# One list that orders the start of an attention and mixture-of-experts kernel, written anew, with freer table changes and later scatters

## The chip, the cores and the metric

The kernel runs on one core of a Trainium2 chip. The metric is device time in microseconds (us) of one execution. Before the change the median of three runs is 699.96 us (699.73 to 700.44). Engine names are those of the profile: PE is TensorE with its matmuls (PEld its weight loads), DVE is VectorE, ACT is ScalarE, POOL is GpSimd, SP is SyncE, which here only issues transfers.

## The reference

Two layers follow each other: a gated linear attention with a complex decay per step, and on its output a mixture of eight experts of which each token takes two.

```python
def _attn_ref(q, k, v, a_re, a_im):            # batch 4, heads 8, steps 768, width 48
    mag = np.sqrt(a_re * a_re + a_im * a_im)
    scale = np.minimum(mag, 0.999) / (mag + 1e-06)
    a_re_n, a_im_n = (a_re * scale, a_im * scale)
    for t in range(S):
        new_re = ar * S_re - ai * S_im         # ar, ai: row t of a_re_n, a_im_n
        new_im = ar * S_im + ai * S_re
        kv = np.einsum('bhd,bhe->bhde', k[:, :, t], v[:, :, t])
        S_re, S_im = (new_re + kv, new_im)
        y[:, :, t] = np.einsum('bhd,bhde->bhe', q[:, :, t], S_re)

def _moe_ref(x, w_gate, w_noise, noise, w1, w2):   # 3072 tokens of 384, 8 experts of 1024
    noisy_logits = x @ w_gate + np.log1p(np.exp(x @ w_noise)) * noise
    top2 = np.argpartition(-noisy_logits, 2, axis=1)[:, :2]
    # softmax over the two logits gives top2_w
    for e in range(E):
        for k in range(2):
            mask = top2[:, k] == e
            h = np.maximum(x[mask] @ w1[e], 0.0)
            out[mask] += top2_w[mask, k, None] * (h @ w2[e])
```

## The kernel before

The attention is done in 24 tiles of 128 steps. Tile `n` is one batch row of one chunk: a chunk has four tiles (its *group* `g = n // 4`), and there are six groups. The decay is turned into a running logarithm and a running angle by matmuls with a triangular matrix (P1 for the angle, P2 for the logarithm), and the matmuls of the attention follow on queries and keys that are scaled and turned by them. The decay inputs come in pairs of tiles, `m = n // 2`; for the first two pairs (`HALVES`, 0 and 1) each step on them is cut into two halves, `a` and `b`.

Each instruction of a tile carries a key: a letter for its engine (A for ACT, D for DVE, P for PE; G for the gates, on all three), a step number, and the tile or pair. The ones that matter here:

- A1, A2, A3, A4 (lines 283 to 290) are the logarithms and exponentials of the decay, D1 to D4 the DVE steps between them (lines 286 to 291); A5 (line 296) is the arctangent, which needs D1 alone among these and must wait until D2 has read the same tile. P1, A6 or D6, D7, D8, A7 and A8 (lines 307 to 326) turn the summed angle into cosine and sine. P2, A9, A10, D9 (lines 331 to 336) scale queries and keys; D10 and D11 (line 344) turn them; P3 and P4 (line 354) transpose them, A11 and A12 (line 355) copy them to `qT` and `kT`. P5 with D12 are the masked scores, P6 with D13 the state, P7 with A13 the output, P8 with A14 its transpose into `xr`.
- G0 to G12 are the gates of a group: the logits, a softplus (G4 to G8a), the two best experts, their weights, and the slots (G10 to G12g) in the expert lists.

The list `ORDER` (line 196) holds these keys up to about the seventeenth tile. `PLACE` (line 754) makes a position of each, which decides the order in which the program is written, and so also the order of transfers on SP and POOL. Lines 849 to 853 bind the keys of each letter to the order of the list: on ACT, on DVE and on PE no instruction of the list may go ahead of the one before it. Work behind the list is placed by due times (`P`, line 750).

ACT holds one table of functions at a time. `phase` (line 244) sorts these instructions into numbered runs, even numbers for the first table and odd ones for the second, and each run begins with a table load. The number comes from group and step alone, whatever the list says; lines 842 to 847 keep the runs apart.

When a group has its slots, POOL scatters its rows to `xs`, two scatters per tile, eight per group (`gate_scatter`, line 492). `PACE` (line 459) lets single scatters wait for A13 of a later tile: `(1, 2): 12` holds tile 2 of group 1 until A13.12 is done. `xr` has three buffers, so POOL's line 404, which opens the buffer of group `g + 3`, waits for the scatters of group `g`. `load_x(0, 0, xga)` (line 804) reads from `xs` the first rows of expert 0 as soon as the groups 0 to 2 are scattered; PE transposes them (line 653) for the first expert's matmuls, which are strewn among the last attention tiles. `psC` has two banks, which P1, P2, P8 and the gates take in turn.

Lines 870 to 932 are the experts, two matmuls per expert with weights split into a high and a low part; they run from about 265 us to the end.

Of the kernel before, what the change touches and what calls it, by code (L numbers as in the profile page):

```python
# [76 lines left out]
def kernel(  # L78
# [103 lines left out]
    for t in ecol:  # L182
# [19 lines left out]
        A10.3 A11.1 D3.3 A4.2 P4.1 D10.2 A4.3 D11.2 P5b.0 A5.2 D12a.0 P6.2 D9.3 P7a.0 D12b.0 A5.3 D5.2 P7b.0
        A12.1 D10.3 P1.4 A13.0 D5.3 P3.2 A6.4 D16.0 D7.4 P5a.1 A11.2 D13.2 P1.5 D4.3 P4.2 D12a.1 A6.5 D4.2 P1.6
        A12.2 D7.5 P7a.1 D11.3 A6.6 P1.7 A8.2 D8.2 P6.3 A6.7 D7.6 A7.2 D7.7 P2.4 D13.3 A8.3 P8.0 D8.3 P5b.1
        A14.0 A7.3 P3.3 D12b.1 A9.4 P5a.2 P7b.1 D12a.2 P5b.2 A10.4 A13.1 D9.4 P2.5 A11.3 D12b.2 P7a.2 A1.4 D10.4
        P8.1 A9.5 P7b.2 D11.4 A2.4 P4.3 A10.5 D1.4 P6.4 A13.2 A14.1 D9.5 P8.2 A12.3 P2.6 D2.4 A14.2 P3.4 A9.6
        D11.5 A3.4 P5a.3 D10.5 A10.6 A11.4 P2.7 D9.6 P5b.3 A1.5 D12a.3 D10.6 P4.4 A9.7 A2.5 D12b.3 P7a.3 A12.4
        D3.4 P7b.3 A10.7 D1.5 P3.5 A13.3 A4.4 D9.7 G0.0 A11.5 D2.5 P5a.4 G1.0 D10.7 P4.5 A3.5 D12a.4 P5b.4 A12.5
        D3.5 P8.3 D12b.4 P3.6 A4.5 D4.4 P5a.5 A14.3 A5.4 D14.0 D16.1 D15.0 G2.0 P5b.5 G3.0 D15.3 G4.0 D15.1
        P7a.4 D12b.5 A5.5 D5.4 P7b.4 D5.5 P1.8 A11.6 D13.4 P1.9 A6.8 D12a.5 A13.4 D7.8 P6.5 A6.9 D4.5 P1.10 D7.9  # L210
        P7a.5 D11.6 A6.10 A8.4 D8.4 P1.11 D11.7 A7.4 P4.6 D15.2 A6.11 P7b.5 D7.10 A12.6 D7.11 P8.4 D8.5 A8.5
# [1 line left out]
        G8a.0 G8b.0 A9.8 G8c.0 G8d.0 A10.8 P7a.6 G8e.0 A12.7 G8f.0 G8g.0 D9.8 P2.9 G9.0 G8h.0 P7b.6 D11.8 A9.9
        A1.6 D10.8 P2.10 A13.6 D13.6 A2.6 P5a.7 G12a.0 G12b.0 A9.10 G12c.0 P3.8 D1.6 A10.9 A10.10 G10.0 D12a.7
        A11.8 P8.6 G12d.0 G11a.0 G12e.0 G12f.0 P5b.7 G11b.0 A14.6 G12g.0 D9.9 P4.8 D12b.7 P2.11 D9.10 A12.8
        P7a.7 D2.6 A1.7 P6.7 D10.9 A9.11 A3.6 P7b.7 D10.10 A2.7 D3.6 P3.9 A13.7 A10.11 D1.7 P5a.8 A11.9 D11.9
        G0.1 A4.6 D12a.8 P5b.8 G1.1 D2.7 P4.9 D13.7 A3.7 P8.7 D12b.8 A12.9 P6.8 D3.7 P8.5 A14.7 D11.10 A4.7
        P3.10 D14.1 D16.2 D15.6 A14.5 P5a.9 D15.4 A5.6 D15.5 G2.1 P7a.8 G3.1 D12a.9 G4.1 P5b.9 D15.7 A5.7 D5.6
        P7b.8 D5.7 P1.12 A11.10 D12b.9 P1.13 D4.7 A6.12 A13.8 P4.10 D7.12 A6.13 D9.11 P1.14 A12.10 D7.13 P7a.9
        D10.11 A6.14 A8.6 P8.8 D7.14 P7b.9 D8.6 A14.8 D4.6 A7.6 P1.15 D13.8 A13.9 P5a.10 A6.15 D7.15 P6.9  # L220
        D12a.10 A8.7 P5b.10 D8.7 D13.9 A7.7 P2.12 D11.11 G5.1 P8.9 D12b.10 P7a.10 A14.9 P3.11 G6a.1 G6b.1 G7.1
        G6c.1 A9.12 G8a.1 P7b.10 G8b.1 A10.12 G8c.1 G8d.1 A11.11 D9.12 P2.13 A13.10 G8f.1 D10.12 P4.11 G9.1
        A9.13 A1.8 G8e.1 P8.10 G12a.1 G8g.1 A10.13 P6.10 G12b.1 G8h.1 G12c.1 A14.10 D9.13 A12.11 G10.1 G12d.1
        P2.14 G11a.1 G12e.1 A2.8 G12f.1 G11b.1 G12g.1 D10.13 P5a.11 A9.14 D11.12 A10.14 P3.12 D9.14 P5b.11
        A11.12 D12a.11 P2.15 D10.14 P7a.11 A1.9 D12b.11 A9.15 P4.12 D13.10 A2.9 D1.8 P7b.11 A12.12 D1.9 P6.11
        A13.11 D2.8 A10.15 P3.13 D11.13 A3.8 P5a.12 D2.9 A11.13 G0.2 D3.8 A3.9 P4.13 D12a.12 G1.2 A4.8 G2.2
        D13.11 P5b.12 G3.2 A12.13 D3.9 P6.12 G4.2 D12b.12 A4.9 P5a.13 D14.2 D11.14 A5.8 P3.14 D12a.13 P5b.13
        D15.8 D4.9 P7a.12 A5.9 D12b.13 P8.11 D5.8 P7b.12 A14.11 D16.3 D15.9 P1.16 D5.9 A11.14 P1.17 D13.12 A6.16
        D15.10 A13.12 P4.14 D7.16 A6.17 D9.15 P7a.13 A12.14 D7.17 P1.18 D10.15 A8.8 P7b.13 D8.8 A6.18 D4.8 A7.8
        P3.15 D7.18 A13.13 P1.19 D15.11 A11.15 P8.12 A6.19 P6.13 A14.12 D7.19 P5a.14 D8.9 A8.9 D11.15 P2.16 A7.9  # L230
        D12a.14 P5b.14 G5.2 D13.13 P7a.14 D12b.14 A9.16 G6a.2 P6.14 G6b.2 G7.2 G6c.2 A10.16 G8a.2 G8b.2 D9.16
        P4.15 G8c.2 P7b.14 D11.16 A12.15 G8d.2 P2.17 A13.14 D13.14 G8f.2 D10.16 P5a.15 G9.2 A1.10 G12a.2 P2.18
        G8e.2 A9.17 A2.10 D12a.15 P3.16 G8g.2 G12b.2 A9.18 G8h.2 G12c.2 D1.10 P7a.15 A10.17 A11.16 G12d.2 D2.10
        G10.2 A10.18 P5b.15 G11a.2 A3.10 G12e.2 G12f.2 G11b.2 G12g.2 P2.19 D9.17 P4.16 D12b.15 A9.19 A1.11 D3.10
        P7b.15 A12.16 D10.17 P8.14 A2.11 D9.18 P6.15 A14.14 P3.17 D1.11 A10.19 A4.10 D11.17 P5a.16 A13.15 D2.11
        P8.13 A11.17 G0.3 D10.18 A3.11 P4.17 D12a.16 G1.3 A14.13 P5b.16 D3.11 A12.17 D13.15 P8.15 A4.11 D14.3
# [865 lines left out]
```

## Time and profile before

| | us |
|---|---|
| median of three runs | 699.96 |
| the profiled execution | 701.72 |
| its span, first to last instruction | 700.0 |
| PE busy in the span | 651.8 (93%) |
| DVE busy | 435.8 (62%) |
| ACT busy | 328.8 (47%) |
| POOL busy | 176.8 (25%) |

The profiled execution is 1.72 us longer than its span, and 1.76 us longer than the median. Shares of the whole span mix two parts: up to about 265 us the attention, in which all engines work, and behind it the experts, in which PE is busy nearly all the time. Matmuls are pipelined and their ends are modelled, so a PE that is shown as busy may still be waiting in part. An instruction on ACT or DVE often begins before the one ahead of it has ended, so a chain of them is shorter than the sum of their durations.

### The profile page before, as it was taken

The numbers are of one execution on the slowest core, as the hardware profiler recorded it, in microseconds if no ns is written. First come the engines' busy times: TensorE is split into PE (matmuls) and PEld (weight loads), VectorE is DVE, ScalarE is ACT, GpSimd is POOL, SyncE is SP. The second block draws the span as 40 slices with busy tenths as digits, with TensorE's granted clock in tenths as the row PEclk, the third lists the DMA queues.
The fourth block names the chain that finished last, engine by engine and source line by source line (L and its number), as shares of the span: only waits on it lengthen the run. The fifth ranks groups of instructions, "written<-read, shape, count | busy, mean of one in ns | idle before, by whom it ended". The sixth has DMA issues, their size and how long they took to land.

```text
span 700.0 us, 13088 instructions
## 1 busy us (share of the span) xinstructions
PE 651.8 (93%) x4970; PEld 577.9 (83%) x4970; DVE 435.8 (62%) x952; ACT 328.8 (47%) x553; POOL 176.8 (25%) x183
## 2 busy tenths in 40 slices
...
GB/s 311 265 206 197 292 164 134 185 198 112 111 68 269 173 140 230 129 55 129 155 90 170 103 126 129 219 63 148 185 56 106 211 77 121 175 23 67 67 35 34
DMA packets 92893, 100.22 MB, mean 143 GB/s; under 512 B 57186, under 2 KB 77013, under 8 KB 92816
## 3 DMA queue, kind: packets, MB, share of 16 engines
...
q0 software_dynamic: 9360, 27.54, 11.3%
...
## 4 chain that ended last, share of the span: by engine, by line
PE 82%; DVE 8%; ACT 5%; DMA 2%; issue 1%; SPq 0%; POOL 0%; POOLq 0%; DVEq 0%; ACTq 0%
PE po L728 28%; PE ph L678 28%; PE psc L363 5%; PE ptr L354 4%; PE pY L412 2%; PE pY L414 2%; PE cum L307 2%; PE psc L678 2%; ACT t L248 2%; PE pG L374 2%; PE po L734 2%; PE cum L427 1%; PE cum L331 1%; DVE qk L336 1%; PE cum L436 1%
## 5 line engine op out<-in xcount | busy, mean ns | idle before, releaser
L728 PE MATMUL po<-w2h,h 128*128 128x384 f32 x768 | 199.8, 338 | 5.7 <-DVE ao L739 5.7
L678 PE MATMUL ph<-x,w1h 128*128 128x512 f32 (+2 forms) x720 | 187.1, 347 | 3.6 <-ACT x L659 3.1
L728 PEld LDWEIGHTS po<-w2h,h 128*128 128x128 f32 x768 | 139.5, 188 | 7.7 <-DVE ao L739 7.7
L678 PEld LDWEIGHTS ph<-x,w1h 128*128 128x128 f32 x720 | 126.3, 189 | 21.4 <-ACT x L659 3.6
L728 PE MATMUL po<-w2l,h 128*128 128x384 f32 x384 | 129.3, 337 | 0.0
L678 PE MATMUL ph<-x,w1l 128*128 128x512 f32 (+2 forms) x360 | 124.7, 346 | 0.0
L740 POOL DMA_INDIRECT out_dram<-ao,ox x52 | 53.5, 1029 | 261.1 <-DVE ao L739 226.1
L497 POOL DMA_INDIRECT xs<-xr,sl x48 | 60.7, 1264 | 202.9 <-DMA ecol<-es 92.8
L684 DVE SCALAR_TENSOR_TENSOR h<-ph,h 128x512 fp32r<-128x512 f32 (+2 forms) x144 | 69.6, 504 | 65.3 <-ACT h L680 59.1
L680 ACT ACTIVATE h<-ph 128x512 fp32r<-128x512 f32 (+2 forms) x120 | 60.2, 508 | 96.8 <-PE ph L678 75.2
L739 DVE SCALAR_TENSOR_TENSOR ao<-po,ex,ao 128x384 f32<-128x384 f32 (+1 forms) x46 | 28.3, 615 | 101.8 <-PE po L728 101.5
L603 ACT CAST w2h<-raw 128x768 fp32r<-128x768 f32 x32 | 26.5, 834 | 112.1 <-PE po L728 87.5
L678 PEld LDWEIGHTS ph<-x,w1l 128*128 128x128 f32 x360 | 67.9, 189 | 8.0
L728 PEld LDWEIGHTS po<-w2l,h 128*128 128x128 f32 x384 | 72.1, 188 | 0.1
L703 POOL DMA_INDIRECT ao<-out_dram,ox x49 | 56.3, 1148 | 44.4 <-issue 24.2
L363 PE MATMUL psc<-qT,kT 112*128 112x128 f32 x384 | 54.3, 283 | 1.1 <-ACT w2h L603 0.6
L363 PEld LDWEIGHTS psc<-qT,kT 112*128 112x128 f32 x384 | 49.2, 196 | 6.0 <-issue 2.0
L659 ACT CAST x<-xt 128x512 fp32r<-128x512 f32 (+1 forms) x42 | 23.0, 551 | 49.1 <-DVE xt L656 46.0
L604 DVE TENSOR_TENSOR w2l<-raw,w2h 128x768 fp32r<-128x768 f32 x32 | 30.3, 955 | 15.3 <-ACT w2h L603 14.5
L414 PE MATMUL pY<-am,v 128*48 128x128 f32 x384 | 38.3, 275 | 1.6 <-DVE am L364 1.6
L364 DVE TENSOR_TENSOR am<-psc,mask 128x512 f32<-128x512 f32 x48 | 32.9, 685 | 9.5 <-PE psc L363 9.1
L412 PE MATMUL pY<-qT,z 112*48 112x128 f32 x320 | 34.2, 279 | 0.2 <-DVE z L397 0.2
(212 smaller groups left out, 927.7 us busy)
## 6 DMA issues: line engine op xcount, KB each, us to landing
...
```

Source lines behind the costliest of these rows:

```text
L363: key(f"P5{'ab'[half]}.{n}", nc.tensor.matmul(p[:, j, :], KT[n][:, h, :], QT[n][:, h, :], start=True, stop=True))
L364: LAST['am'] = nc.vector.tensor_mul(AM[n][:, 4 * half:4 * half + 4, :], p, mask[:, None, :].to_broadcast([128, 4, 128]))
L412: x = nc.tensor.matmul(o, Z[b][:, h, :], QT[n][:, h, :], start=True, stop=False, skip_group_check=True)
L414: x = nc.tensor.matmul(o, V[n][:, h, :], AM[n][:, h, :], start=not g, stop=True, skip_group_check=True)
L497: d = nc.gpsimd.indirect_dma_start(out=xs, out_offset=bass.IndirectOffsetOnAxis(ap=sl[:, kk, b:b + 1], axis=0), in_=XR[g][:, lo + b, :], i ...
L604: d = nc.vector.tensor_tensor(lo, raw_t, hi.bitcast(F32), op=OP.subtract)
L678: LAST['m'] = nc.tensor.matmul(p[:, :c], W1[e, kk][i][:, f * 128:(f + 1) * 128], XW[w, kk][:, j, 0:c], start=(m == 0), stop=(m == len(ms) ...
L680: nc.scalar.activation(h[:, 0:c], p[:, :c], AF.Relu)
L684: LAST['h'] = nc.vector.scalar_tensor_tensor(h[:, dst:dst + b - a], p[:, a:b], 0.0, h[:, a:b].bitcast(F32), op0=OP.max, op1=OP.subtract)
L703: nc.gpsimd.indirect_dma_start(out=ao[j][0:w, :], out_offset=None, in_=out, in_offset=bass.IndirectOffsetOnAxis(ap=OX[e][0:w, j:j + 1], ax ...
L728: LAST['po'] = key(f"PO.{e}.{j}", nc.tensor.matmul(p[:, :DM], HT[w, f][i][:, o:o + 128], W2[f // 2][k2][:, f % 2, :], start=(m == 0), stop ...
L740: d = nc.gpsimd.indirect_dma_start(out=out, out_offset=bass.IndirectOffsetOnAxis(ap=OX[e][0:n, j:j + 1], axis=0), in_=a, in_offset=None, b ...
```

## The change

Five things change.

1. `ORDER` is a new list. It has 717 keys instead of 710 and reaches to P7 and D12 of tile 17. Of the old list's keys it lacks five (D10.18, P3.18, D13.15, D15.15, P6.16).
2. The runs of tables follow the list: each key gets the number of the run in which the list puts it, and a new run begins wherever the list goes from one table to the other. By the list the first pair's work now has five runs where it had three: logarithms and exponentials, the four arctangents, the rest of the exponentials, the sines, and then the exponentials of the next tiles. Two table loads are added, 15 instead of 13.
3. `PACE` holds tile 1 of group 1 until A13.13 (was 11), tiles 2 and 3 until A13.15 (12 and 13), tiles 1 and 2 of group 2 until A13.16 (15), tile 3 until A13.17 (16).
4. The first pair's decay inputs come as one transfer each instead of two halves.
5. The softplus tiles have two buffers instead of one.

```diff
-    c, w, u = (pool.tile(shape, F32, name=tag + x) for x in "cwu")
+    c, w, u = (pool.tile(shape, F32, name=tag + x, bufs=2) for x in "cwu")
...
-        A1a.0 A2a.0 D1a.0 A1b.0 D2a.0 A2b.0 A3a.0 D1b.0 D3a.0 D2b.0 A4a.0 A3b.0 D4a.0 A1a.1 D3b.0 P2.0 A2a.1
...
-        P5a.6 D13.5 A7.5 P6.6 D12a.6 A14.4 G5.0 P3.7 P5b.6 A11.7 G6a.0 G6b.0 P2.8 G6c.0 D12b.6 G7.0 A13.5 P4.7
...
+        A1a.0 A1b.0 A2a.0 A2b.0 D1a.0 D1b.0 D2a.0 A1a.1 D2b.0 A3a.0 A2a.1 D3a.0 A1b.1 D1a.1 A4a.0 D2a.1 A2b.1
+        D4a.0 A5a.1 D1b.1 P2.0 D2b.1 A5a.0 A5b.1 P1.0 A5b.0 A9.0 D6.0 D7.0 A3b.1 A10.0 D3b.1 A3b.0 P1.1 D9.0
...
+        P8.4 P5a.6 A14.4 G5.0 P6.5 D12a.6 P5b.6 D13.5 A9.8 G6a.0 A11.7 D11.7 P6.6 A10.8 D12b.6 P7a.6 G7.0 G6b.0
...
-    def phase(i, *args, **kw):
-
+    def usual(k):
+        a, i = k.split(".")
+        a, i = a.rstrip("ab"), int(i)
+        if a[0] == "G":
+            return 2 * min(i + 3, NG)
+        if a in ("A9", "A10"):
+            return 2 * (i // B) + 2 if i > 1 else 0
+        return 2 * (2 * i // B) + (a in ("A5", "A7", "A8"))
+
+    RUN, run, last = {}, 0, None
+    for k in ORDER:
+        if k.split(".")[0].rstrip("ab") in ("A1", "A2", "A3", "A4", "A5", "A7", "A8", "A9", "A10", "G5", "G7", "G9"):
+            run += (usual(k) - run) % 2
+            RUN[k], last = run, k
+    shift = run - usual(last)
+
+    def phase(name, *args, **kw):
+        i = RUN.get(name, usual(name) + shift)
...
-        for j in range(2) if m == 0 else (slice(0, 2),):
-            nc.sync.dma_start(RE[m][:, j], a_in[m, 0][:, j])
-            nc.sync.dma_start(IM[m][:, j], a_in[m, 1][:, j])
+        nc.sync.dma_start(RE[m], a_in[m, 0])
+        nc.sync.dma_start(IM[m], a_in[m, 1])
...
-        key(f"A1{x}.{m}", phase(ph, ta, re, AF.Ln))
+        key(f"A1{x}.{m}", phase(f"A1{x}.{m}", ta, re, AF.Ln))
...
-    PACE = {(0, 1): 8, (0, 2): 9, (0, 3): 10, (1, 1): 11, (1, 2): 12, (1, 3): 13, (2, 1): 15, (2, 2): 15, (2, 3): 16,
+    PACE = {(0, 1): 8, (0, 2): 9, (0, 3): 10, (1, 1): 13, (1, 2): 15, (1, 3): 15, (2, 1): 16, (2, 2): 16, (2, 3): 17,
             (3, 1): 18, (3, 2): 19, (3, 3): 19, (4, 0): 20, (4, 1): 20, (4, 2): 21, (4, 3): 22}
```

Three places show how the instructions now stand. Line numbers grow by 13 to 16 with the change.

On ACT, around the first table changes, `t00`, `t01` and `t02` are the three work tiles of a pair (201 to 203 and 221 to 223 before, 199 to 201 and 220 to 222 now), `ee` the factors that A9 and A10 make. Before, from the A4 of the first pair's second half:

```order
L248 ACTIVATE t01_202<-t00_201,b_eps_79 128x384
L248 ACTIVATE t01_222,bad_101<-t00_221 128x384
L248 ACTIVATE t01_222<-t01_222 128x384
L248 ACTIVATE ee_234<-cum_232 128x384 x2
L248 ACTIVATE t01_222<-t00_221,b_eps_79 128x384
L248 ACTIVATE t01_222<-t01_222 128x384
L248 ACTIVATE ee_251<-cum_249 128x384 x2
L248 ACTIVATE t01_222<-t00_221,b_eps_79 128x384
L247 ACT_TABLE_LOAD
L248 ACTIVATE t02_203<-t02_203 128x384
L248 ACTIVATE t02_223<-t02_223 128x384 x2
L248 ACTIVATE t02_203<-t02_203 128x384
```

The same place on ACT now:

```order
L264 ACTIVATE t01_221,bad_101<-t00_220 128x384
L263 ACT_TABLE_LOAD
L264 ACTIVATE t02_222<-t02_222 128x384
L264 ACTIVATE t02_201<-t02_201 128x384
L264 ACTIVATE t02_222<-t02_222 128x384
L264 ACTIVATE t02_201<-t02_201 128x384
L263 ACT_TABLE_LOAD
L264 ACTIVATE ee_243<-cum_241 128x384
L264 ACTIVATE t01_221<-t01_221 128x384
L264 ACTIVATE ee_243<-cum_241 128x384
L264 ACTIVATE t01_200<-t01_200 128x384
L264 ACTIVATE t01_221<-t00_220,b_eps_79 128x384
```

The four arctangents (`t02`) stood behind all logarithms and exponentials of the two pairs and behind the factors of two tiles; now they stand ahead of three of the four A3, three of the four A4 and all factors, with a table load on either side.

On ACT, a little later, from the table load ahead of the second pair's logarithms on; `qT` and `kT` are the transposed queries and keys that the scores need. Before (`qT` of tile 0 stands ahead of this piece):

```order
L247 ACT_TABLE_LOAD
L248 ACTIVATE t00_347<-re_160 128x768
L248 ACTIVATE ee_291<-cum_289 128x384
L248 ACTIVATE t01_348,bad_101<-t00_347 128x768
L248 ACTIVATE t00_389<-re_164 128x768
L248 ACTIVATE ee_318<-cum_316 128x384
L248 ACTIVATE t01_390,bad_101<-t00_389 128x768
L355 ACTIVATE kT_358<-ptr_359 112x1024
```

Now:

```order
L263 ACT_TABLE_LOAD
L264 ACTIVATE ee_286<-cum_284 128x384 x2
L264 ACTIVATE t00_336<-re_158 128x768
L368 ACTIVATE qT_323<-ptr_324 112x1024
L264 ACTIVATE t00_359<-re_162 128x768
L264 ACTIVATE t01_337,bad_101<-t00_336 128x768
L368 ACTIVATE kT_370<-ptr_371 112x1024
L264 ACTIVATE ee_299<-cum_297 128x384
L264 ACTIVATE t01_360,bad_101<-t00_359 128x768
L264 ACTIVATE ee_299<-cum_297 128x384
L264 ACTIVATE ee_349<-cum_347 128x384
L368 ACTIVATE qT_404<-ptr_405 112x1024
```

`kT` of tile 0 no longer stands behind the factor `ee_318`, the fourth tile's, which reuses the first tile's buffer.

On POOL, the scatters of the groups 1 to 3; `xr_924`, `xr_1432` and `xr_2014` are these groups' rows before. Before:

```order
L404 MEMSET xr_2014 128x4x7
L405 COPY xr_2014<-tokid_89 128x4
L497 DMA xs<-xr_924,sl4_1726 24576x400 x8
L404 MEMSET xr_2496 128x4x7
L405 COPY xr_2496<-tokid_89 128x4
L497 DMA xs<-xr_1432,sl4_2299 24576x400 x8
L404 MEMSET xr_3146 128x4x7
```

Now, where the same groups are `xr_917`, `xr_1360` and `xr_1891`:

```order
L417 MEMSET xr_1891 128x4x7
L418 COPY xr_1891<-tokid_89 128x4
L510 DMA xs<-xr_917,sl4_2070 24576x400 x4
L510 DMA xs<-xr_1360,sl4_2235 24576x400 x2
L510 DMA xs<-xr_917,sl4_2070 24576x400 x4
L417 MEMSET xr_2471 128x4x7
L418 COPY xr_2471<-tokid_89 128x4
L510 DMA xs<-xr_1360,sl4_2235 24576x400 x6
L417 MEMSET xr_3146 128x4x7
```

Two scatters of group 2 now stand ahead of the last four of group 1, and the last two of group 2 are bound to A13.17.

## Rows read from the trace of the kernel before

**Rows 1.** Busy time of each engine in five stretches (counts in brackets), clock, transfers.
```profile
core 0: us, PE busy (x) PEld busy (x) DVE busy (x) ACT busy (x) POOL busy (x), PEclk, DMA share, GB/s
0.00:4.50 4.50, 0.00 (x0) 0.00 (x0) 2.19 (x17) 2.42 (x4) 3.83 (x19) 1.00 0.50 129
4.50:41.80 37.30, 19.97 (x125) 12.91 (x126) 28.70 (x53) 28.35 (x49) 1.58 (x10) 0.86 0.83 267
41.80:75.70 33.90, 33.69 (x380) 27.62 (x380) 31.42 (x49) 31.63 (x49) 0.00 (x0) 1.00 0.77 238
75.70:186.90 111.20, 108.63 (x1386) 88.46 (x1386) 103.76 (x241) 93.61 (x151) 32.16 (x26) 1.00 0.57 173
186.90:262.00 75.10, 69.82 (x749) 58.96 (x747) 54.64 (x176) 43.13 (x77) 20.76 (x20) 1.00 0.47 154
```

**Rows 2.** Timeline of the start: start, duration, instruction, in brackets the wait before it.
```profile
0.83 0.40 SPq L258 DMA_DIRECT2D re<-in_a_dram  x1
3.31 0.52 ACT L248 ACTIVATE t<-re 128x384 f32<-128x384 f32 x1 [1.21 <-DMA re<-in_a_dram]
5.60 0.52 ACT L248 ACTIVATE t<-re 128x384 f32<-128x384 f32 x1 [1.11 <-DMA re<-in_a_dram]
15.04 1.28 ACT L247 ACT_TABLE_LOAD   x1
16.33 1.76 ACT L248 ACTIVATE t<-t 128x384 f32<-128x384 f32 x4
16.91 5.16 PE L307 MATMUL cum<-t,tri_t 128*128 128x384 f32 x8 [3.59 <-ACT t L248]
18.59 0.56 DVE L315 TENSOR_SCALAR tf<-cum 128x384 f32<-128x384 f32 x1 [2.35 <-PE cum L307]
24.15 1.06 PE L354 MATMUL ptr<-ident,qh 128*112 128x128 f32 x8 [0.51 <-DVE qh L344]
25.72 1.82 DVE L344 TENSOR_TENSOR kh<-qk,tr 128x768 f32<-128x768 f32 x2
34.60 1.01 ACT L355 ACTIVATE kT<-ptr 112x1024 f32<-112x1024 f32 x1
35.67 1.95 PE L354 MATMUL ptr<-ident,qh 128*112 128x128 f32 x8 [6.15 <-ACT kT L355]
40.51 1.28 ACT L247 ACT_TABLE_LOAD   x1
...
40.96 0.68 DVE L364 TENSOR_TENSOR am<-psc,mask 128x512 f32<-128x512 f32 x1
41.56 0.95 DVE L336 TENSOR_TENSOR qk<-qk,ee 128x768 f32<-128x768 f32 x1
```

**Rows 3.** The stretch behind PE's longest gap, columns as in the first group.
```profile
35.60:38.00 2.40, 2.33 (x11) 2.33 (x12) 2.37 (x5) 2.40 (x6) 0.00 (x0) 0.50 0.21 4
```

**Rows 4.** Groups by line: count, busy us and mean ns, idle time before them.
```profile
L247 ACT ACT_TABLE_LOAD x13 | 16.7, 1283 | 0.9 <-PEq L1089 0.8
```

**Rows 5.** What DVE waited for between 75 and 187 us: total, times, longest.
```profile
DVE ga4u L40 <- ACT ga4w L248: 1.6, 1, 1.6
```

**Rows 6.** A stretch of 20 us in the middle, columns as in the first group.
```profile
150.00:170.00 20.00, 19.22 (x220) 14.75 (x219) 17.73 (x48) 16.05 (x26) 6.47 (x6) 1.00 0.36 110
```

**Rows 7.** Timeline of POOL, SP, ACT and PE around group 2's last scatters.
```profile
191.16 1.22 POOL L497 DMA_INDIRECT xs<-xr,sl  x1 [6.08 <-ACT xT L419]
...
195.44 0.34 SPq L541 DMA_DIRECT2D xga<-xs  x1
...
198.46 1.28 ACT L247 ACT_TABLE_LOAD   x1
201.65 0.60 ACT L419 ACTIVATE xT<-pY 128x512 f32<-128x512 f32 x1
...
209.49 0.38 PE L653 MATMUL ptr<-ident,xga 128*128 128x128 f32 x1
...
222.80 3.17 POOL L497 DMA_INDIRECT xs<-xr,sl  x1 [6.58 <-ACT xT L419]
```

More of the change, by code (lines that the diff above doesn't have):

```diff
@@ L202 @@
[L202 to L211, printed above, removed]
@@ L212 @@
-        P5a.6 D13.5 A7.5 P6.6 D12a.6 A14.4 G5.0 P3.7 P5b.6 A11.7 G6a.0 G6b.0 P2.8 G6c.0 D12b.6 G7.0 A13.5 P4.7
[L213 to L236, printed above, removed]
@@ new lines @@
+        P4.0 D10.1 A2.2 P6.1 A12.0 D1.2 A9.2 D13.1 P3.1 A2.3 D2.2 P5a.0 A10.2 D1.3 A9.3 A11.1 P5b.0 D12a.0 A3.2
+        D2.3 P4.1 A10.3 D12b.0 P7a.0 A3.3 D3.2 P7b.0 A12.1 D3.3 A4.2 P5a.1 D9.2 A4.3 P5b.1 D4.2 A13.0 D11.2 A5.2
+        P8.0 D10.2 P6.2 D12a.1 P3.2 A14.0 D5.2 A5.3 P7a.1 D13.2 P1.4 A11.2 D5.3 P1.5 A6.4 D9.3 P4.2 A6.5 D7.4
+        D7.5 P1.6 A12.2 D11.3 P1.7 A8.2 D10.3 P6.3 A6.6 D8.2 A6.7 D7.6 P3.3 A7.2 D7.7 D16.0 P2.4 D8.3 A8.3
+        D12b.1 P5a.2 A7.3 D4.3 P7b.1 A9.4 D12a.2 P5b.2 D13.3 P2.5 D12b.2 A13.1 A10.4 P7a.2 A11.3 D9.4 P8.1 P7b.2
@@ new lines @@
+        A9.5 D11.4 A14.1 P4.3 A10.5 D10.4 A13.2 P6.4 A1.4 D9.5 P8.2 A12.3 P2.6 D10.5 A2.4 P3.4 D11.5 A14.2 P5a.3
+        D1.4 A11.4 P5b.3 D2.4 A9.6 A10.6 P2.7 D12a.3 A3.4 D12b.3 P4.4 A9.7 D9.6 A1.5 P7a.3 D3.4 A12.4 P7b.3
+        D10.6 A13.3 P3.5 A2.5 D11.6 G0.0 A11.5 D1.5 P5a.4 A4.4 D2.5 P4.5 G1.0 A10.7 D4.4 P5b.4 A3.5 D12a.4 A12.5
+        G2.0 P8.3 D3.5 A14.3 P3.6 D12b.4 A4.5 G3.0 D14.0 P5a.5 G4.0 D15.0 A5.4 D4.5 P7a.4 D12a.5 P5b.5 D15.2
+        A5.5 D5.4 P7b.4 D5.5 P1.8 A11.6 D13.4 P1.9 D15.3 A6.8 D15.1 A13.4 P4.6 D7.8 A6.9 D12b.5 P1.10 A12.6 D7.9
@@ new lines @@
+        P7a.5 D9.7 A6.10 A8.4 D8.4 P1.11 D10.7 A7.4 P7b.5 D7.10 A6.11 D16.1 P3.7 A13.5 D7.11 D8.5 A8.5 P2.8 A7.5
+        P8.4 P5a.6 A14.4 G5.0 P6.5 D12a.6 P5b.6 D13.5 A9.8 G6a.0 A11.7 D11.7 P6.6 A10.8 D12b.6 P7a.6 G7.0 G6b.0
+        D9.8 P2.9 G6c.0 D10.8 P7b.6 A1.6 G8a.0 D11.8 A9.9 P4.7 A13.6 G8b.0 D13.6 A10.9 P2.10 G8c.0 A12.7 G8d.0
+        D9.9 P8.6 A9.10 P6.7 G8f.0 A14.6 D10.9 A10.10 P5a.7 G9.0 D11.9 A2.6 P3.8 D12a.7 P2.11 G8e.0 A11.8 D9.10
+        P5b.7 A9.11 D1.6 A1.7 P7a.7 D12b.7 A10.11 A2.7 P4.8 D2.6 P7b.7 D1.7 A12.8 P8.5 D10.10 A13.7 P3.9 A3.6
@@ new lines @@
+        D2.7 P5a.8 A14.5 A11.9 D3.6 P8.7 D13.7 P5b.8 A3.7 D12a.8 A14.7 P4.9 D3.7 A4.6 P6.8 D12b.8 A4.7 D14.1
+        D16.2 G0.1 D15.4 A12.9 D11.10 P7a.8 G1.1 D4.7 A5.6 G2.1 P7b.8 G3.1 D15.5 G4.1 D9.11 P3.10 A13.8 D5.6
+        P5a.9 A5.7 D13.8 A11.10 P8.8 D5.7 P1.12 A14.8 D10.11 P5b.9 A6.12 G12a.0 D7.12 P1.13 G12b.0 D12b.9 P4.10
+        A6.13 G12c.0 D12a.9 P1.14 D7.13 A12.10 G8g.0 D4.6 P7a.9 A6.14 G12d.0 A8.6 G8h.0 P1.15 D7.14 G12e.0 D8.6
+        G10.0 A6.15 D15.7 P3.11 A7.6 G11a.0 D7.15 G12f.0 G11b.0 P5a.10 A8.7 G12g.0 D8.7 D15.6 A7.7 P6.9 D12a.10
```

52 lines of the change are left out of this document (32 added, 20 removed).

## The prediction

> **What bounds the kernel now.** I read the busy times by stage first, then the timeline of the first 42 us, then the waits of DVE in the middle, and last the timeline around 190 to 210 us, where the attention feeds the experts. The stages [rows 1] are cut at ACT's changes to the trigonometric table. From 41.80 to 75.70 DVE is busy for 31.42 of 33.90 us and ACT for 31.63; from 75.70 to 186.90 DVE for 103.76 of 111.20 and ACT for 93.61. PE reads 108.63 there, but its matmuls are pipelined, so that a PE that reads busy may wait; its weight loads take 88.46. So DVE bounds the attention from about 40 us on, with ACT close to it, and its idle time from 41.8 to 186.9 is 2.48 + 7.44 = 9.9 us in all. In the start, 4.5 to 41.8, DVE is busy for 28.70 of 37.30 us: 8.6 us idle. Behind 187 us DVE falls to 54.64 of 75.10 and PE (69.82) leads, up to the end. The reader is to see that there are two places where a new order can gain, 8.6 us in a short start and 9.9 us thinly spread over 145, and that the experts after it run on PE and gain nothing of their own.
>
> The start [rows 2]: ACT waits for its first input to 3.31, its second half comes at 5.60. The first run of the exponential table has 20 steps (the keys of the list) and lasts until the table load at 15.04: 11.73 / 20 = 0.59 us a step, waits included. The four arctangents take 1.76, the first summed angle starts at 16.91 and DVE reads it at 18.59. The keys of tile 0 reach `kT` only at 34.60, and PE has waited 6.15 us when it goes on at 35.67, at half its clock: the granted clock is 0.50 (the 1.2 GHz level) from 35.6 to 38 [rows 3]. Eight transposes take 1.95 us there, and 1.06 at 24.15 [rows 2].
>
> **The change, part by part.**
>
> The start. I walk the new list with these durations. One transfer of the pair instead of two halves: the first step can begin neither before 3.31 (half the data) nor much after 5.60 (all of it and the rest behind it); I take the middle, 4.5, later by 1.2. The first run now has 10 steps: 10 x 0.59 = 5.9, load at 10.4. Load 1.28, four arctangents 1.76, load 1.28: 14.7. The angle sum starts 0.58 behind the arctangents' start (16.91 - 16.33), at about 12.5, and reaches DVE 1.68 later (18.59 - 16.91), at 14.2, where before it was 18.59. Eight steps of the exponential table at 0.59 follow: load at 19.4, sines from 20.7. On DVE, D9.0 follows A10.0 (about 16.1) with 0.87 (two such instructions take 1.82, so one starts 0.87 behind the other), then twelve steps of half size at about 0.5 (an estimate from the 0.56 of one): the first turned key, D11.0, at 23.1. The last sine needs the twelfth of them and ends at 24.1 and the fifth table is in by 25.4. ACT then has two factors, A1.2, `qT`, A1.3 and A2.2: half-size steps at 0.44 (four take 1.76), full ones at twice that, a copy at 1.0, 4.5 together and somewhat less where they overlap. `kT` of tile 0 starts at about 29.7, 5 us before its old 34.60. Up to the next arctangents come thirteen steps, counted in the same way some 9.3 us: load at 39.0, the arctangents at 40.3, where their table load alone began at 40.51 before.
>
> The lead at that point is counted on DVE, since DVE bounds what follows. By the list, when DVE has finished D10.2 it has done all that it had done before at 41.56 [rows 2], and D12b.0 (0.60) and D4.2 (0.87) besides. From D1.2, which follows A2.2 at 29.6, to D10.2 it has thirteen steps: ten of full size at 0.87, two D12 at 0.6 (41.56 - 40.96), one D13 at 0.5, 10.4 us, and I find 0.1 of waiting: 40.1. Lead: 41.56 - 40.1 + 1.47 = 2.9 us. Two further table loads (2.56) are inside this walk. They cost nothing beyond it because DVE has its twelve steps while ACT loads; without that cover they would cost all of it. Bounds: with the input at 5.60 the walk is 1.1 later and the lead 1.8; with it at 3.4 the lead is 4.0; with PE at half clock until the first scores it falls to about 1 (below).
>
> What the softplus buffers and the other edits to `phase` do, beside the order, is to allow it: they add no instruction. Two issues fewer on SP (0.40 each) lie in the start, where SP is not waited for.
>
> The middle. The same instructions stand in another order, so DVE's busy time stays and only its 9.9 us of idle time can change. One wait is named by the trace and dealt with by the list: G6a waits 1.6 us for the softplus's first exponential [rows 5]; now D12a.6 and D13.5, 0.6 + 0.5, stand in between. I take -1.1. Bounds: half of all idle time goes (-5); or DVE idles throughout as it did between 150 and 170, 2.27 of 20 us [rows 6], which over 145 us makes 16.5 (+6.6). The value is the only one with a row of its own.
>
> The scatters. Group 2's last pair was held for A13.16, started at 191.16, and SP read `xs` for expert 0 at 195.44, 4.28 later [rows 7]. It is now held for A13.17. That stood 3.2 behind the table load at 198.46; the list puts more ahead of it (eight factors, one `kT`, two gate steps): 1.28 + 8 x 0.4 + 1.0 + 0.2 = 5.7 behind, the 0.4 an estimate from the 0.44 above. With its own 0.6 it is done at 204.8 on the old clock. Plus 4.28: SP reads at 209.1. A load took 2.5 us from issue to use at the start (0.83 to 3.31) [rows 2], so the rows are there at 211.6 or a little later. PE first wants them at 209.49, in the new program behind about 0.8 us more work: 210.3. So PE, in order, waits 1.3 to 2 us; what queues behind it are the scores of tile 19 and the gates of group 4, on which DVE and ACT wait. Bounds: 0 (the wait falls into pauses that PE has here anyway: it idles 5.3 of 75.1 us from 187 to 262) and 2.8 (all of it, and a slower load). I take 1.0. POOL itself has room: A13.15, which frees group 1's last scatters, stands in the list ahead of the arctangents at 186.9, and the transpose of tile 16, which wants their buffer, behind the table load at 198.46.
>
> Sum: -2.9 - 1.1 + 1.0 = -3.0 us. On the profiled execution's own 701.72 this is 698.7; the median lies 1.76 below that execution, so 699.96 - 3.0 = 697.0.
>
> **A rule on table loads.** The trace has 13 loads of 1283 ns with no wait of note around them [rows 4], and the arctangents start 1.29 behind the load's start [rows 2]. The Trainium skill (ScalarE: Activation LUTs, "What ACT_TABLE_LOAD costs") gives 1283 ns for the load, as here, and a drain of 1380 ns besides, 2.66 us a switch. By it the two new loads would cost 2.8 us more than in my walk and leave a lead of 0.1. No row here shows such a drain.
>
> **The rivals.**
>
> *The late read of `xs` decides; slower.* Place: POOL's last pair of group 2, SP's read, PE's transposes. For it: nothing else stands between A13.17 and the read, and one scatter can take 3.17 instead of about 1 [rows 7], which adds 2. Price: 2.8 + 2 = 4.8; it decides from 4.3 on (the lead and 1.4), and without the -1.1 gives 699.96 - 2.9 + 4.8 = 701.9. Against it: most scatters in the trace are of the short kind, and the lead shifts both sides alike.
>
> *The middle gets worse; slower.* +6.6 as above: 703.7. For it: the lists are strict, and late gate steps (G10 to G12g of group 0 now stand among tile 10's work) tie DVE to PE and ACT at more places. Against: DVE has less idle time here than anywhere else.
>
> *A deeper gain in the middle.* Half of the idle time goes: 699.96 - 2.9 - 5 + 1 = 693.
>
> *PE at half clock in the start.* The angle sums are few; if PE is still slow at 28 us, then the groups P4.0, P6.1, P3.1 and P5.0 take 1.9 us instead of about 1 [rows 2, 3], end at 35.5, and DVE loses 1.9: lead 1.0, time 698.9. The row speaks for it only behind a gap of 6 us. The Trainium skill (TensorE: Matmul & The Clock Gate, part 1) says that the slow clock is the default and steady activity lifts it, which would speak for this case; at 24.15 the trace shows eight transposes at 1.06 after a start just as thin.
>
> *Nothing left of the lead; no change.* Either the two new loads lie on the path after all, 2.56, lead 0.3: 699.96 - 0.3 - 1.1 + 1.0 = 699.6. Or what follows 187 us is held by a chain that the start doesn't move: 699.9. For the first: ACT is nearly as full as DVE. (The rule above would make it worse still.) Against both: DVE, not ACT, has the fewest pauses from 41.8 on, and the weights that the experts load wait for buffers of the attention.
>
> **How the numbers follow.** Forecast 0.45 (its own range 695.3 to 698.7), deeper gain 0.15, half clock 0.12, nothing left 0.13 (0.03 for the loads), late read 0.08, worse middle 0.07. A measurement of this kernel can tell 0.2%, 1.4 us, from no change. Faster: 0.42 of the forecast, 0.15, and 0.04 of the half clock: 0.61. Slower: the two slower cases and 0.02 of the lost lead: 0.17. Same: 0.22. The range leaves out the far ends on either side: 693.2 to 701.6.
>
> **What would show it.** Right: the third trigonometric run's arctangents (the first on full tiles) at about 40; `kT` of tile 0 before 31; no stretch at 0.50 before 45; PE transposing `xga` right after a wait of 1 to 2 us. The lead then shows unchanged at each table load, and at 187. Wrong: first logarithm after 5.6; DVE's idle time from 41.8 to 187 above 11 us; an idle PE of over 3 us before the transposes; or a lead at 187 that is gone at 300.

## The result, and the profile after

The changed kernel takes 707.88 us (705.66 to 712.72, four runs) against 700.2 beside it: a ratio of 1.011 (1.007 to 1.016). It is slower by 7.7 us; 697.0 was forecast, with 693.2 to 701.6 as the range. The profiled execution took 708.81 with a span of 707.1.

The start went as forecast. The timeline of ACT in the new trace, to be read against [rows 2] (start, duration, instruction, in brackets the wait before it; rows picked out of it):

```profile
3.96 0.94 ACT L264 ACTIVATE t<-re 128x384 f32<-128x384 f32 x2 [1.85 <-DMA re<-in_a_dram]
9.56 1.28 ACT L263 ACT_TABLE_LOAD   x1
12.63 1.28 ACT L263 ACT_TABLE_LOAD   x1
18.36 1.28 ACT L263 ACT_TABLE_LOAD   x1
23.31 1.28 ACT L263 ACT_TABLE_LOAD   x1
29.69 1.01 ACT L368 ACTIVATE kT<-ptr 112x1024 f32<-112x1024 f32 x1
38.49 1.28 ACT L263 ACT_TABLE_LOAD   x1
```

The walk had 4.5, 10.4, 13.4, 19.4, 24.1, 29.7 and 39.0 for these rows. The load at 38.49 answers to 40.51 before, and `kT` of tile 0 comes 4.9 us sooner.

The stages in the new trace, columns and cuts as in [rows 1] from its second row on:

```profile
4.50:41.80 37.30, 25.59 (x212) 16.51 (x212) 30.99 (x57) 34.61 (x59) 1.60 (x10) 1.00 0.85 278
41.80:75.70 33.90, 32.37 (x340) 25.64 (x335) 32.72 (x52) 31.41 (x48) 0.00 (x0) 1.00 0.74 229
75.70:186.90 111.20, 104.67 (x1339) 86.34 (x1339) 100.22 (x239) 91.99 (x147) 23.66 (x22) 0.98 0.54 162
186.90:262.00 75.10, 65.97 (x689) 55.07 (x686) 52.49 (x165) 40.93 (x72) 24.78 (x22) 1.00 0.49 159
```

Up to 75.7 DVE has done 2.29 + 1.30 = 3.6 us more work than before, and no stretch of the start is at half clock. From 75.7 to 186.9 it does 3.5 us less than before, so that nothing of the lead is left at 186.9; from 186.9 to 262 it does another 2.2 less, and PE 3.9 less. So the lead is there and is lost behind 75.7 us, at more places than one. The largest hole, in steps of 2 us, same columns:

```profile
174.00:176.00 2.00, 2.00 (x35) 1.95 (x30) 2.00 (x3) 1.84 (x3) 0.39 (x1) 1.00 0.20 38
176.00:178.00 2.00, 2.00 (x32) 1.81 (x34) 2.00 (x5) 1.99 (x4) 1.70 (x2) 1.00 0.24 89
178.00:180.00 2.00, 1.76 (x35) 1.37 (x24) 2.00 (x6) 0.72 (x1) 1.58 (x2) 1.00 0.46 176
180.00:182.00 2.00, 0.00 (x0) 0.00 (x0) 0.49 (x2) 0.16 (x1) 1.09 (x1) 1.00 0.36 138
182.00:184.00 2.00, 1.84 (x31) 1.72 (x33) 1.65 (x4) 1.98 (x3) 0.96 (x2) 0.72 0.21 75
184.00:186.00 2.00, 2.00 (x14) 1.64 (x11) 0.63 (x3) 1.82 (x3) 0.00 (x0) 0.50 0.00 0
```

From 180 to 182 no matmul of PE is on record; behind the hole its granted clock falls to 0.50 (the 1.2 GHz level). Who waited there, in the view of waits (total, times, longest):

```profile
ACT lt L453 <- remote: 3.1, 1, 3.1
DVE am L377 <- remote: 1.5, 1, 1.5
```

`lt` is the copy of the gate logits of group 3, `am` the masked scores; both read what PE had computed by 179.8, by its modelled ends, and they start at 181.84 and 181.94. "remote" says that the profile has no releaser on this core's rows. PE's results came late, with nothing shown that PE waited for.

The late read, answering to [rows 7], in rows of ACT, POOL, SP and PE:

```profile
204.85 0.63 ACT L432 ACTIVATE xT<-pY 128x512 f32<-128x512 f32 x1
205.75 0.97 POOL L510 DMA_INDIRECT xs<-xr,sl  x1 [10.92 <-ACT xT L432]
207.03 1.11 POOL L510 DMA_INDIRECT xs<-xr,sl  x1 [0.30 <-issue]
209.84 0.34 SPq L554 DMA_DIRECT2D xga<-xs  x1
214.28 1.43 SPq L625 DMA_DIRECT2D raw<-in_moe_w_dram  x3
214.67 0.50 PE L666 MATMUL ptr<-ident,xga 128*128 128x128 f32 x2 [1.78 <-DMA xga<-xs]
```

A13.17 (forecast to end at 204.8, it ends at 205.5) releases the last pair, SP reads 4.1 us after the first of the pair starts, and PE gets the rows 4.8 us behind the read, where 2.5 was taken. The weights of the first expert (`raw`) stand behind the read on SP.

### The profile page after: what moved, and what is told of

Read it like the earlier page. It is cut to its first block, busy times and chain, and to the rows that moved or that the text cites. A ratio compares the mean times of both kernels' runs of the same rounds, so it can differ in the third digit from the quotient of the medians.

```text
span 707.1 us, 13083 instructions
## 1 busy us (share of the span) xinstructions
PE 655.8 (93%) x4970; PEld 579.1 (82%) x4970; DVE 435.8 (62%) x952; ACT 331.6 (47%) x555; POOL 175.0 (25%) x183
## 4 chain that ended last, share of the span: by engine, by line
PE 73%; DVE 7%; ACT 6%; issue 6%; DMA 5%; POOL 1%; SPq 0%; POOLq 0%; DVEq 0%; ACTq 0%
PE po L741 28%; PE ph L691 26%; PE ptr L367 3%; PE psc L376 3%; PE cum L321 2%; PE pY L427 2%; PE pY L425 2%; DMA out_dram<-ao,ox 1%; ACT t L264 1%; PE pG L387 1%; PE psc L691 1%; PE po L747 1%; POOL xs L510 1%; PE cum L440 1%; PE cum L345 1%
## 5 line engine op out<-in xcount | busy, mean ns | idle before, releaser
L691 PE MATMUL ph<-x,w1h 128*128 128x512 f32 (+2 forms) x720 | 189.2, 350 | 3.1 <-ACT x L672 2.8
L510 POOL DMA_INDIRECT xs<-xr,sl x48 | 56.3, 1174 | 209.1 <-DVE z L410 112.4
L377 DVE TENSOR_TENSOR am<-psc,mask 128x512 f32<-128x512 f32 x48 | 32.6, 683 | 12.0 <-PE psc L376 10.4
```

The costliest lines, as they stand in the source:

```text
L377: LAST['am'] = nc.vector.tensor_mul(AM[n][:, 4 * half:4 * half + 4, :], p, mask[:, None, :].to_broadcast([128, 4, 128]))
L510: d = nc.gpsimd.indirect_dma_start(out=xs, out_offset=bass.IndirectOffsetOnAxis(ap=sl[:, kk, b:b + 1], axis=0), in_=XR[g][:, lo + b, :], i ...
L691: LAST['m'] = nc.tensor.matmul(p[:, :c], W1[e, kk][i][:, f * 128:(f + 1) * 128], XW[w, kk][:, j, 0:c], start=(m == 0), stop=(m == len(ms) ...
```

## The experiments

The kernel before was run beside each set, and it showed two kinds of chip: it takes 695.8 to 696.3 us on chips 5 and 11, and 701.2 to 702.0 on chips 2, 6 and 14. The first result (700.2 for the kernel before) is counted with the second kind, since its trace shows the same wait as after_c's (below). All ratios are to the kernel before on the same chip, with the 95% interval.

**The waits put back, in part or whole.** Edits of the changed kernel's `PACE`: group 2 alone (late_read_back), both groups (pace_back), both but the last pair (last_pair); and the kernel before with the new ones (pace_only).

```
 late_read_back  -(2, 1): 16, (2, 2): 16, (2, 3): 17      +(2, 1): 15, (2, 2): 15, (2, 3): 16
 pace_back       also -(1, 1): 13, (1, 2): 15, (1, 3): 15  +(1, 1): 11, (1, 2): 12, (1, 3): 13
 last_pair       as pace_back, but (2, 3): 17
```

> The changed kernel with group 2's three waits put back to the copies of tiles 15, 15 and 16; nothing else differs. Theory 1 (the late read): the last scatter of group 2 starts some 13 us sooner, at about 193 instead of 207, SP reads xs before 197, PE no longer waits for it, and of the 8.1 us lost between 183 and 222 us at least the 4.8 of the read come back: 702.5 to 703.5. Theory 2 (the new list itself loses it from tile 13 to tile 20, the read only joins in): the time stays within 1.5 us of 707.9, and the copy of tile 19 still stands after 225.

Measured on chip 11: 1.0007 (0.9989 to 1.0024). The changed kernel itself did not lose on this chip (1.0002, below), so there was no loss to give back. But beside pace_back, of the same chip (0.9971, next), it says that group 2's waits put back alone bring nothing, although SP reads early again and PE does not wait for the rows:

```profile
192.82 0.34 SPq L554 DMA_DIRECT2D xga<-xs  x1
...
205.56 0.61 PE L666 MATMUL ptr<-ident,xga 128*128 128x128 f32 x3
```

> The changed kernel with all six changed waits of groups 1 and 2 put back. Theory 1: as with group 2's alone, 702.5 to 703.5, since group 1's slots are not what the first read waits for. Theory 2: about 707.9. If group 1's waits matter by themselves (its scatters stood at 167 to 184 us, beside a stall of all engines at 180), it is faster than the run with group 2's alone by 2 us or more.

0.9971 (0.9955 to 0.9988) on chip 11, 0.36% below late_read_back: group 1's waits cost time by themselves, which theory 1 had ruled out. And again on chip 5:

> The changed kernel with the old waits, again: 0.9971 was measured. Theory (the late read costs 2 to 3 us of a lead of 2.5): 0.996 to 0.998 again, and 0.003 to 0.004 below after_again beside it. If the first result repeats for after_again, the gap between the two shows how much of it the waits explain: all of it would be 0.014.

0.9979 (0.9963 to 0.9996), the changed kernel beside it 1.0012: the six waits cost 0.33%, 2.3 us (the two intervals just touch).

> As pace_back, but the one wait of group 2's last pair on the copy of tile 17 kept. Theory: SP reads xs for expert 0 about 13 us later than in pace_back, at 203 instead of 189, as in the full change, and the time is that of after_again within 0.7 us. Rival (the crowding of scatters, not the read): the time is that of pace_back.

1.0006 (0.9989 to 1.0023) on chip 5: 1.9 of the 2.3 us come with this one wait, though its interval overlaps that of pace_back_again. In its trace SP reads at 203.49 and PE waits 1.1 us for the rows; in that of pace_back (chip 11) the weights no longer stand right behind the read and PE does not wait for it:

```profile
189.36 0.34 SPq L554 DMA_DIRECT2D xga<-xs  x1
...
202.37 0.42 SPq L625 DMA_DIRECT2D raw<-in_moe_w_dram  x1
...
205.60 0.61 PE L666 MATMUL ptr<-ident,xga 128*128 128x128 f32 x3
```

> The kernel before with the six new waits alone; its list, table runs, loads and buffers are the old ones. Theory 1: A13.17 stands at 201.65 there, so the last pair goes out at about 202.5, SP reads at 206.6 and the rows land at 209 to 211 where PE wants them at 209.5: 1 to 5 us slower, 701 to 705. Theory 2: no change, 699.7 to 700.7.

1.0025 (1.0008 to 1.0042) on chip 11, 1.7 us; and on chip 14, of the second kind:

> The old kernel with the new waits alone: 1.0025 on the other chip, by the late read. If the late read is all that the waits do on any chip: 1.002 to 1.004. If spreading the scatters spares stalls here: 1.000 or below.

1.0024 (1.0003 to 1.0045). With the old list the six new waits cost the same 1.7 us on either kind of chip. That they cost time is shown, and it is about a quarter of the loss of the first result. That they cost it by the late read alone is not shown: with the new list on the first kind of chip, group 1's waits cost as much with an early read (late_read_back) as the late read does without them (last_pair), and all six cost no more (1.0002 and 1.0012, below). The traces divide it otherwise. The last A13 of the attention in pace_back, late_read_back and after_here, all on chip 11:

```profile
253.39 0.60 ACT L432 ACTIVATE xT<-pY 128x512 f32<-128x512 f32 x1 [0.71 <-PE pY L427]
254.08 0.60 ACT L432 ACTIVATE xT<-pY 128x512 f32<-128x512 f32 x1 [0.71 <-PE pY L427]
256.01 0.60 ACT L432 ACTIVATE xT<-pY 128x512 f32<-128x512 f32 x1 [0.71 <-PE pY L427]
```

By these, group 1's waits cost 0.7 us and group 2's 1.9. Each is one execution; which division holds stays open.

**The changed kernel again, on other chips.** Kernels unchanged.

> The changed kernel once more, unchanged, beside the others of this set. Theory 1 and 2 expect the same ratio as first measured, 1.007 to 1.016; with late_read_back at 1.0007 the late scatters of group 2 are then worth 0.6 to 1.5%. A third theory (the first result was of its chip: stalls of all engines there at 127 and 180 us): the ratio is below 1.005 and the trace shows no stall of all engines at 180.

1.0002 (0.9981 to 1.0023) on chip 11: the loss isn't there. The third theory's condition holds, and the trace has no hole. The stretch that answers to the one above stands 2 us sooner:

```profile
174.00:176.00 2.00, 1.92 (x29) 1.51 (x31) 2.00 (x4) 1.72 (x4) 1.69 (x2) 1.00 0.04 14
176.00:178.00 2.00, 2.00 (x44) 1.61 (x33) 2.00 (x6) 1.95 (x4) 1.70 (x2) 1.00 0.52 202
178.00:180.00 2.00, 2.00 (x40) 1.81 (x37) 2.00 (x4) 1.97 (x3) 1.25 (x2) 1.00 0.32 114
```

> The kernel before, unchanged, for a trace of the same chip as the others; ratio 1.000 within 0.002. It gives the size of the difference that two equal kernels show here.

0.9999 (0.9979 to 1.0018) on chip 11: what two equal kernels differ by.

> The changed kernel a third time. First measured at 1.0114 (1.0066 to 1.0161), then on a second chip at 1.0002 (0.998 to 1.002). If the loss belongs to the chip on which it ran first, this comes out at 1.011 where the kernel before takes about 700, and at 1.000 where it takes about 696.

1.0012 (0.9995 to 1.0029) on chip 5.

> The changed kernel where the kernel before takes some 702 us and old_start took 1.0228. There PE stood still behind matmuls of the gates with nothing that the profile shows to wait for (at 168 to 174 us five times 1.14 to 1.23 us). If these stalls are the chip's, and what the first result adds to the late read: 1.009 to 1.016. Where the kernel before takes 696: 1.000 to 1.002.

1.0100 (1.0066 to 1.0134) on chip 14: the first result again. In its trace the same copy `lt` waits 3.1 us for "remote". So the loss goes with the kind of chip, and the next experiments ask which part of the change meets it.

**Which part of the list.** new_start and new_half take the new list up to and with A5.2 (some 40 us) or A5.6 (some 105 us by the trace; the expectation below has 135), then the old order; old_start and old_half the other way round; old_order has the old list with the rest of the change. All have the old waits.

```
 ORDER of new_start = new[: "A5.2"] + [k for k in old if k not in that part]
 ORDER of old_start = old[: "A5.2"] + [k for k in new if k not in that part]
```

> The old list and the old waits, with the rest of the change: table runs by the list (the same 13 loads), pair 0 in one load, softplus in two buffers. By the prediction's walk the one load starts ACT 0.7 to 1.2 us later and nothing else counts: 1.000 to 1.002.

0.9996 (0.9980 to 1.0011) on chip 5: the other edits cost nothing that can be measured.

> The new list up to the arctangents of pair 2 (some 40 us), the old order of everything else behind it, the old waits; table runs by the list, pair 0 in one load. The lead was 2.0 us at that table load. Theory 1 and 2 alike: the start keeps its lead, 696 to 698.5. Rival (what follows 187 us is held by a chain that the start does not move): 699.5 to 700.5.

0.9985 (0.9970 to 1.0000) on chip 11: 1.0 us of the start's lead arrives. In its trace A13 stands 1.6 us ahead of the kernel before on the same chip in the middle (77.26 against 78.85) and 1.2 at the end of the attention (254.43 against 255.61). On chip 14:

> The new list up to 40 us only, old order and old waits behind it. If the stalls come with the new order of the gate steps from tile 9 on: 0.998 to 1.000, as on the other chip. If they come with any change of the program: above 1.005.

0.9989 (0.9967 to 1.0011): much as on the other kind, 0.8 us, though not told from no change.

> The new list up to the arctangents of pair 6 (some 135 us), the old order behind it, the old waits. If the lead of 4 to 5 us that the new list has at 130 us is carried to the end, the ratio is 0.993 to 0.995; if what follows 187 us holds the end, it is that of new_start, 0.9985, or above it.

0.9987 (0.9968 to 1.0007) on chip 11: no more than new_start. ACT waits 5.4 us for PE right behind the seam, and from tile 9 on its copies stand within 0.03 us of those of the kernel before (119.69 against 119.66). The new list's table loads ran 4.9 us ahead at the seam (104.65 against 109.57); I read it so that the list had put off other work, which was then due. With no lead left in the trace the ratio still reads 0.9987, so a tenth of a per cent here is not told from nothing.

> The old order up to the arctangents of pair 6, the new list behind it, the old waits: no lead from the start. If the new list loses time between tile 9 and tile 17 (theory 2), the ratio is 1.003 to 1.007; if it loses none there, 0.999 to 1.001.

1.0010 (0.9992 to 1.0029) on chip 11: not told from no change.

> The old list up to the arctangents of pair 2 (some 40 us), the new list for everything behind it, the old waits. new_start, its counterpart, took 0.9985 and both parts together (pace_back) 0.9971 and 0.9979. If the gain is the start's alone: 0.999 to 1.001 here. If the new middle gains by itself (the prediction's 1.1 us): 0.998. If the new list behind the start costs something that only its own start pays for: 1.001 to 1.004.

1.0228 (1.0196 to 1.0260), on chip 6 (second kind): 16 us, far beyond every theory. And the whole list with the old waits on chip 14:

> The same with the old waits. If on such a chip the stalls come when the scatters of a group go out in one row (8 from 162 to 172 us in old_start, whose list behind the start is the same): 1.015 or more, above after_c, so that the new waits are a help there. If the late read decides there as well: 0.003 to 0.005 below after_c. Where the kernel before takes 696: 0.997 to 0.998.

1.0138 (1.0087 to 1.0189), where new_start_c has 0.9989: on this kind of chip the list behind the start costs 1.5%, 10 us. The rival of the late read fell here: pace_back_c is not below after_c. The theory of scatters in one row has its sign, above after_c, but not its 1.015; and whether the new waits help there in time (by 0.4%) stays open, since the intervals overlap. The place of the largest hole, PE's rows in pace_back_c, at the slots of group 2 (G10.2; the expectation of gates_back takes them for group 1's, which stand at 153.99):

```profile
164.20 0.17 PE L492 MATMUL cum<-ohs,tri_b 128*128 128x8 bf16 x1
165.42 0.17 PE L490 MATMUL cum<-ohs,ones_b 128*128 128x8 bf16 x1 [1.05 <-issue]
166.16 0.17 PE L490 MATMUL cum<-ohs,ones_b 128*128 128x8 bf16 x1 [0.57 <-issue]
166.86 0.18 PE L490 MATMUL cum<-ohs,ones_b 128*128 128x8 bf16 x1 [0.53 <-issue]
168.28 0.17 PE L492 MATMUL cum<-ohs,tri_b 128*128 128x8 bf16 x1 [1.24 <-issue]
168.31 0.17 PE L490 MATMUL cum<-ohs,ones_b 128*128 128x8 bf16 x1
169.00 0.17 PE L490 MATMUL cum<-ohs,ones_b 128*128 128x8 bf16 x1 [0.53 <-issue]
169.71 0.22 PE L490 MATMUL cum<-ohs,ones_b 128*128 128x8 bf16 x2 [0.54 <-issue]
```

"issue" is time in which PE waited for nothing shown. The first and the last of the eight scatters of group 1 that stand beside it, and a stretch of the hole, columns as in [rows 1]:

```profile
158.30 0.99 POOL L510 DMA_INDIRECT xs<-xr,sl  x1 [18.15 <-DVE am L377]
...
167.37 0.97 POOL L510 DMA_INDIRECT xs<-xr,sl  x1 [0.30 <-issue]
...
168.00:170.00 2.00, 0.66 (x6) 0.43 (x6) 0.00 (x0) 0.26 (x1) 0.33 (x1) 0.50 0.34 128
```

With the new waits, which break up that row, the slots of group 2 have no hole on the second kind of chip either. In the first result (and likewise at 163.25 in after_c):

```profile
163.03 0.18 PE L492 MATMUL cum<-ohs,tri_b 128*128 128x8 bf16 x1 [0.26 <-DVE ohs L481]
...
163.30 0.24 PE L490 MATMUL cum<-ohs,ones_b 128*128 128x8 bf16 x4
```

pace_back_c's kernel in the trace of chip 11 (pace_back) has these matmuls in one piece, in a row of eight scatters too:

```profile
161.45 0.17 PE L492 MATMUL cum<-ohs,tri_b 128*128 128x8 bf16 x1
161.48 0.22 PE L490 MATMUL cum<-ohs,ones_b 128*128 128x8 bf16 x3
161.55 0.17 PE L492 MATMUL cum<-ohs,tri_b 128*128 128x8 bf16 x1
161.58 0.24 PE L490 MATMUL cum<-ohs,ones_b 128*128 128x8 bf16 x4
```

**The gates put back.** pace_back with 26 keys of the gates of groups 0 and 1 where the old list has them; in the list:

```
 ... G9.1 A13.10 P2.14 D13.10 A12.11 D9.13 P8.10
+G12a.1 G8g.1 G12b.1 G8h.1 G12c.1 G10.1 G12d.1 G11a.1 G12e.1 G12f.1 G11b.1 G12g.1
 A9.14 P5a.11 D2.8 ...
```

> The new list with the last gate steps of groups 0 and 1 (G8e, G8g, G8h, G10 to G12g, 26 keys) put back to where the old list has them, two tiles earlier; the old waits. Theory (the gates' new place makes the stalls: PE's small gate matmuls of group 1 stand at 165 to 170 us beside eight scatters in one row): on a chip where the kernel before takes 700 to 702 the hole of 5 to 7 us at these matmuls goes and the ratio falls from 1.0138 (pace_back_c) to 1.003 to 1.007. Rival (any dense stretch of small matmuls of the new list stalls there, wherever the gates are): 1.010 or more. On a chip where the kernel before takes 696: 0.996 to 0.998, as with the old waits alone.

1.0069 (1.0043 to 1.0096) on chip 2 (second kind), at the upper end of the theory's 1.003 to 1.007 and below the rival's 1.010. Half of pace_back_c's 1.38% is gone, if two chips of one kind may be compared. Its waits:

```profile
ACT lt L453 <- remote: 6.0, 2, 3.5
PEld L490 <- issue: 0.3, 1, 0.3
```

The hole at the slots of group 2 is gone; those at the logits (`lt`) stay, so each theory has half. But it is not the gates' place that did it there: group 2's gate steps were not moved. What moved away from them are group 1's scatters, which no longer go out in one row of eight but in pairs from 133.27 on, the last pair at 164.03; the slots of group 2 stand at 167.30 in one piece.

## Why the prediction was wrong

**The start, -2.9: right in its course, too large at the end.** Every time of the walk came within 1.1 us, and DVE was ahead by 2.3 us of work at 41.8. Alone it is worth 0.8 to 1.0 us, and both intervals reach 1.000. A part of the lead belongs to the one execution it was counted in: on chip 11 the kernel before does 29.47 us of DVE work from 4.5 to 41.8, not 28.70. The two added table loads did no harm that shows: each takes 1283 ns, and the arctangents start 1.29 us behind the load's start (38.49 to 39.78). A drain besides, as the Trainium skill has it (ScalarE: Activation LUTs, "What ACT_TABLE_LOAD costs"), is in no row of the new trace either.

**The middle, -1.1: this is the step that failed.** It said that DVE's busy time stays and only its 9.9 us of idle time can change, and took the one named wait; it gave PE no stop of its own. That wait did go: `ga4u` is no longer among DVE's waits. But DVE's idle time from 41.8 to 186.9 rose to 1.18 + 10.98 = 12.2 us. On chip 11, where PE has no holes, the same subtraction gives 8.4 for the kernel before and 6.3 for the changed one, a gain of 2.1. The rows there, first of the kernel before:

```profile
41.80:75.70 33.90, 33.12 (x349) 26.74 (x347) 31.42 (x50) 31.66 (x49) 0.00 (x0) 1.00 0.78 246
75.70:186.90 111.20, 109.64 (x1411) 89.91 (x1407) 105.30 (x244) 94.62 (x152) 33.42 (x26) 1.00 0.56 168
```

and of the changed one:

```profile
41.80:75.70 33.90, 32.44 (x340) 25.64 (x339) 32.78 (x51) 31.49 (x48) 0.00 (x0) 1.00 0.78 225
75.70:186.90 111.20, 109.80 (x1406) 89.90 (x1404) 106.07 (x248) 94.43 (x152) 26.61 (x24) 1.00 0.54 163
```

So the reasoning on DVE holds on one kind of chip. On the other PE stands still behind small matmuls of the gates, all engines wait for it, and the new list behind the start costs 10 us with the old waits. The rival "the middle gets worse" had the sign and was given 0.07. That it pointed at gate steps is in part luck: it named the slots of group 0 (G10 to G12g), and the first result's largest hole stands at the logits of group 3. Its price, 6.6, came from DVE's pauses and was too small, and its 703.7 leaves out the +1.0 of the scatters (704.7 with it).

**The late read, +1.0: right in its wait, too small in its cost, and not all that the new waits do.** PE waits 1.8 us, where 1.3 to 2 was forecast. The six waits cost 1.7 us with the old list and 2.3 with the new, 1.9 of it with the last pair's alone. Three parts were not in the sum: the rows land 4.8 us behind the read, not 2.5; the weights of the first expert stand behind it on SP (4 us later on chip 11: 207.88 in after_here, 203.68 in late_read_back); and group 1's waits, for which the prediction saw room on POOL, take away the gain by themselves in late_read_back.

**The tail.** Of what the prediction listed as wrong, two came: an idle DVE of over 11 us, and a lead at the table load of 182.96 (2.6 us) that is gone at the next (199.16 against 198.46). PE's wait of 1.8 us before the transposes is one of the signs that it listed as right. The last 2 us are lost between 290 and 320, where PE has 0.86 of its clock from 300 on; the kernel before has such a stretch on chip 11 (0.83 from 280 to 290), so these 2 us are not shown to be the change's.

Split by the runs, the change is on the first kind of chip -1.0 (start) - 0.7 (the rest of the list: 0.9975, the mean of two runs, less new_start) + 2.3 (waits) = +0.6 us, each term uncertain by some 1.2 us or more; on the second -0.8 + 10.4 (1.0138 less 0.9989) - 2.7 (the waits, not settled) = +6.9, with some 3.5 us of uncertainty in the last two.

**What stays open.** Why PE stands still on chips 2, 6, 14 and the first. The holes go with rows of scatters on POOL: the slots of group 2 have one in pace_back_c (eight scatters from 158.30 to 168.34) and in old_start (162.33 to 172.38), and none where that row is broken up, in the first result, after_c and gates_back; and the copy `lt` of the first result waits in a row of four (175.61 to 181.28). But such a row is not enough: on chip 11 it stands beside the same matmuls without a hole (pace_back, 155.55 to 166.81), and in the kernel before on the first chip group 3's `lt` starts at 182.68, in a row from 178.95 to 185.08, without a wait. The Trainium skill (Runtime: NRT & Kernel Launch, "Instruction fetch mechanics") says that instructions arrive in blocks of 16 KiB, mostly hidden. The page of the profile has such packets, `q8 instruction: 45, 0.74, 0.4%`, 16 KB each, but the view of queues lists none from 175 to 182 us, so no run here shows that the hole is one of them.

The version to keep: new_start loses on neither kind of chip (0.9985, 0.9989), and its gain is at the edge of what can be measured; pace_back gains more on one (0.9971, 0.9979) and loses 1.4% on the other.
